# First batch's scores from K and Q as they arrive, splits by halves ahead of the masks, scores of every second slot copied in two

## The chip, the cores and the metric

The kernel runs on one core of a Trainium2 chip, in one launch. The metric is the device time of that core in microseconds (us). Beside the timed runs there is one execution recorded by the hardware profiler; all rows below are from that one. Its engines are TensorE (PE, with PEld for weight loads), VectorE (DVE), ScalarE (ACT), GpSimd (POOL) and SyncE (SP), which issues the transfers.

## The reference

Attention over 8 batches and 8 heads, 576 tokens, 64 dimensions, in which each query keeps only its 32 highest scores, and then a gated chain of matrix products over all 4608 tokens. All inputs are fp32.

```python
scores = (q @ k.transpose(0, 1, 3, 2)) / sqrt(64)        # B=8, H=8, S=576
kth    = np.partition(scores, -32, axis=-1)[..., -32:-31]
scores = np.where(scores >= kth, scores, -1e9)
attn   = np.exp(scores - scores.max(-1, keepdims=True))
attn   = attn / (attn.sum(-1, keepdims=True) + 1e-9)
x      = (attn @ v).transpose(0, 2, 1, 3).reshape(4608, 512)
a, b   = x @ w1, x @ w2                                   # 512 x 1024 each
out    = ((a * b) @ w3) @ w_out                           # 1024 x 1024, 1024 x 512
```

## The kernel before

The work is cut into 144 slots, 18 per batch. A slot is 128 queries of a pair of heads (a few are 64 queries of two pairs), so its scores are a tile `s` of 128 x 2 x 576. Twelve slots give a block of 384 tokens, on which the chain of products runs (tiles `ab` for x@w1 and x@w2, `g` for their product, `eo` for the output; w3 @ w_out is folded into `wf` once, in the first slots).

fp32 accuracy on TensorE is kept by splitting: an operand is written as a high part in fp32r and a low part, the rest, and three products (high-high, low-high, high-low: `PARTS`) stand for one. Q and K come from memory as fp32 into a buffer `raw`, of which there are two, and GpSimd splits them with two instructions into `qt` or `kt`: a CAST for the high part and a TENSOR_TENSOR for the low one (`split_next`, line 218). `load_q` and `load_k` only note what is wanted, `load_next` (line 211) issues the transfer, `load_ahead` (line 223) keeps two under way. A `qt` holds 256 columns and serves two slots, a `kt` 576. Slot 0 alone is scored from the bare fp32 Q and K (`first`, line 613), in one product.

All engines run in the order in which the program is written: a helper class pins every instruction, which is why every row of the profile has its one line, L64, and rows are told apart by the tiles' names. The main loop (line 644) runs over steps p. In a step stand:

- VectorE: the fold of slot p, two tensor_tensor w<-s and two w<-w,s, then top-32 by rounds of MAX8 and MATCH_REPLACE8; the low parts of `x`; the products a * b.
- GpSimd: `edge` and `sums`, then for slot p-1 two masks `pab<-s,pab`, the first of which waits for the last instruction of VectorE's fold; behind the masks the low parts of `g` that are due and one or two splits of a raw Q or K (line 673); in the first slots parts of the weights' decoding.
- ScalarE: the step functions `pab<-s,edge` in front of the masks, the exponentials `pab,sums<-pab,edge`, the normalising `pab<-pab,sums`, and copies out of PSUM (`banks`), the scores' own among them (`take_scores`, line 273).
- TensorE: transposes (`banks<-ident,pab`) and values (`banks<-pab,vt`) of slot p-3, the scores of slot p+2, and in between the chain's products, 12 at a time (`fill`, `SHARES`).

Once the first block has started, the scores of two slots are made in one even step, in two regions of one PSUM tile (`BASES`). The second slot's scores lie in a region that the transposes use too, and are copied in the odd step already (`ahead`, line 711), between the two exponentials. `s` has three buffers. A batch's K is asked for when the last slot that reads the same pair of heads of the batch before is scored (`renew`, line 576).

Of the kernel before, what the change touches and what calls it, by code (L numbers as in the profile page):

```python
# [46 lines left out]
SHARES = (0, 12, 0), (12, 12, 12)  # L47
BASES = (768, 1728), (2304, 192)
TURNED, HOMES = 1024, (0, 2880)
PARTS = (0, 0), (1, 0), (0, 1)  # L50
Q = 256

# [22 lines left out]
def attn_moe(ctx: ExitStack, tc: tile.TileContext, q, k, v, w1, w2, w3, w_out, out, flag, any_missed, general):  # L75
# [120 lines left out]
    def at(x, b, *i):  # L196
        return x[(b, *i)] if isinstance(b, int) else x[(ds(b, 1), *i)].rearrange("o p n -> (o p) n")
# [1 line left out]
    wanted, raws, now = [], [], [0]  # L199

    def load_q(b, t, half):
        qt = att_p.tile([128, 2, Q], F32R, tag="q", name="qt")
        wanted.append((qt, at(q, b, t)[:, half * Q : (half + 1) * Q]))
        return qt

    def load_k(b, hp):
        kt = kv_p.tile([128, 2, S], F32R, tag="k", name="kt")
        wanted.append((kt, at(k, b, hp)))
        return kt

    def load_next():
        to, src = wanted.pop(0)
        raw = raw_p.tile([128, S], F32, tag="raw", name="raw")
        raw = raw[:, : to.shape[-1]]
        sp.dma_start(raw, src)
        raws.append((now[0], raw, to))

    def split_next(engine):
        _, raw, to = raws.pop(0)
        engine.tensor_copy(to[:, 0, :], raw)  # L220
        engine.tensor_tensor(to[:, 1, :], raw, to[:, 0, :].bitcast(F32), op=ALU.subtract)

    def load_ahead():
        while wanted and len(raws) < 2:
            load_next()

    def ready(*tiles):
# [10 lines left out]
    def products_of(cuts, qt, kts, hps):  # L238
        parts = PARTS if qt.dtype == F32R else PARTS[:1]
        for n, (i, j) in enumerate(parts):  # L240
            for a, (dst, lo, hi) in enumerate(cuts):
                rows = HEADS[hps[0] % 2 ^ a] if len(hps) == 1 else slice(0, 128)
                c = (hps[0] + (a if len(hps) == 2 else 0)) * 128 % Q
                pe.matmul(
                    dst, qt[rows, i, c : c + 128], kts[hps[0] // 2 * 2 + a][rows, j, lo:hi],
                    start=n == 0, stop=n == len(parts) - 1,
                )
# [10 lines left out]
    def scores_whole(qt, kts, hps, i):  # L258
        ready(qt, *(kts[hps[0] // 2 * 2 + a] for a in range(2)))
        banks, cuts = late["banks"][:, :], [[], []]  # L260
        for base in BASES[i]:
            n = 512 - base % 512
            for lo, hi in ((0, n), (n, S)):
                cuts[hi - lo < HS].append((banks[:, base + lo : base + hi], lo, hi))
        for cut in cuts:
            products_of(cut, qt, kts, hps)
        apart = BASES[i][1] - BASES[i][0]
        return bass.AP(banks.tensor, banks.offset + BASES[i][0], [banks.ap[0], [apart, 2], [1, S]])

    def new_s():  # L270
        return att_p.tile([128, 2, S], F32, tag="s", name="s", bufs=S_BUFS)

    def take_scores(s, st):
        if not isinstance(st, list):
            act.copy(s, st)
            return
        for src, (lo, hi) in list(zip(st, HALVES))[::-1]:
            act.copy(s[:, :, lo:hi], src[:, :, :HS])

    def top32_steps(s, slot):  # L280
        w = att_p.tile([128, 2, S], F32, tag="w", name="w", bufs=1)
# [291 lines left out]
    def of(table, b):  # L573
        return {hp: table[b, hp] for hp in range(NHP) if (b, hp) in table}

    def renew(table, load, i, last):
        b, hps, _ = slots[i]
        for hp in range(NHP):
            if last[b, hp] == i and b + 1 < B:
                table[b + 1, hp] = load(b + 1, hp)  # L580

    halves, half_at = [], []
    for b, hps, t in slots:
# [4 lines left out]
    def renew_q(g):  # L588
        if g < len(halves):
            qts[g] = load_q(*halves[g])  # L590
# [19 lines left out]
        prefetch(WAITING)  # L610

    now[0] = -4
    first = z_p.tile([128, 3 * CHUNK], F32, tag="z", name="z")
    bare = [first[:, o : o + n].rearrange("p (i c) -> p i c", i=1) for o, n in ((0, S), (S, S), (2 * S, Q))]
    sp.dma_start(bare[2][:, 0], at(q, 0, 0)[:, :Q])
    sp.dma_start(bare[0][:, 0], at(k, 0, 0))
    stir(6)
    prefetch(1)
    sp.dma_start(bare[1][:, 0], at(k, 0, 1))
    for hp in (2, 3):  # L620
        kts[0, hp] = load_k(0, hp)
    prefetch(2)
    load_next()
    prefetch(4)
    load_next()
    renew_q(1)
    for hp in (0, 1):
        kts[0, hp] = kv_p.tile([128, 2, S], F32R, tag="k", name="kt")
    turned, ovs = {}, {}

    def put_back(m):
# [1 line left out]

    def score(h, st):
        b, hps, t = slots[h]
        sts[h] = st(qts[half_at[h]], of(kts, b), hps) if half_at[h] else st(bare[2], bare, hps)

    def scored(h):
        renew(kts, load_k, h, last_pair)
# [4 lines left out]
    for p in range(-2, n_slots + 4):  # L644
        h, i, j, l, m = p + 2, p + 1, p - 1, p - 2, p - 3
        now[0] = p
        if p == 1:
            vts[0, 0] = load_v(0, 0)
            vts[0, 1] = load_v(0, 1)
            vts[0, 2] = load_v(0, 2)  # L650
            vts[0, 3] = load_v(0, 3)
        finder = top32_steps(ss[p], p) if 0 <= p < n_slots else iter(())
        if 0 <= i < n_slots and i not in ss:
            ss[i] = new_s()
            take_scores(ss[i], sts[i])
        for part in fresh:
            split_high(*part)
        if 0 <= j < n_slots:
            edges[j] = edges_of(j)
        if 0 <= l < n_slots:  # L660
            add_up(pabs[l][1])
        folded = next(finder, None)
        for part in fresh:
            split_low(*part)
        fresh.clear()
        take_lasts()
        warm()
        if 0 <= j < n_slots:
            pabs[j] = new_weights()
            for a in range(2):  # L670
                mask(ss[j], edges[j], pabs[j][0], a, folded if a == 0 else None)
        take_lows()
        for _ in range(2 if len(raws) + len(wanted) > 3 else 1):
            if raws and raws[0][0] < p:
                split_next(pool)
        if p == 0:
            raws[:0] = [(-4, bare[hp][:, 0], kts[0, hp]) for hp in range(2)]
        load_ahead()
        warm()
        begin()  # L680
        if p % 2:
            fill(SHARES[1][0])
            evict()
        next(finder, None)
        if 0 <= m < n_slots:
            turned[m] = take_turned(pabs[m][0], *turn(pabs[m][0], None if late else sts[i][1]))
        take_held()
        take_lows()
        if 0 <= l < n_slots:
            invert(pabs[l][1])  # L690
            normalise(*pabs[l])
        if 0 <= j < n_slots:
            exps(edges[j], *pabs[j], 0)
        warm()
        if p == 3:
            stir(6)
        fill(SHARES[p % 2][1])
        next(finder, None)
        warm()
        if h not in sts and (not late or h % 2) and h < n_slots:  # L700
            score(h, (lambda *a: scores_whole(*a, 1)) if late else scores)
            scored(h)
        elif h % 2 == 0:
            for n in (h + 1, h):
                if n < n_slots:
                    score(n, lambda *a, n=n: scores_whole(*a, n % 2))
            for n in (h, h + 1):
                if n < n_slots:
                    scored(n)
        load_ahead()  # L710
        ahead = late and p % 2 == 1 and h < n_slots and h in sts
        if ahead:
            ss[h] = new_s()
            take_scores(ss[h], sts[h])
        if 0 <= j < n_slots:
            exps(edges[j], *pabs[j], 1)
        if 0 <= m < n_slots:
            if not put_back(m):
                for n in [m - 1, m] if put_back(m - 1) else [m]:
                    b, hps, t = slots[n]  # L720
                    ovs[n] = values(of(vts, b), hps, turned.pop(n), n < m)
                    renew(vts, load_v, n, last_use)
        if p == 14:
            stir(9)
        next(finder, None)
        warm()
        for _ in finder:
            pass
        if p % 2:
            hold.append(True)  # L730
        fill(SHARES[p % 2][2])
        hold.clear()
        for d in sorted(ovs):
            b, hps, t = slots[d]
            n = d // BLOCK
            for hp in hps:
                if (n, hp) not in xs:
                    xs[n, hp] = new_x(n)
            fresh += parts_of([xs[n, hp] for hp in hps], column[group_of[d]], t, ovs.pop(d))
            del ss[d], pabs[d], edges[d], sts[d]  # L740
            if (d + 1) % BLOCK == 0:
                starting.append(n)
        if p == 2:
            stir(8)
        warm()
# [73 lines left out]
```

## Time and profile before

| | before |
|---|---|
| time, median of 3 runs (lowest to highest) | 1291.63 us (1289.79 to 1291.91) |
| profiled execution, time | 1289.22 us |
| profiled execution, span | 1287.4 us |
| mean granted TensorE clock | 0.971 of full speed |
| TensorE busy | 1196.6 us (93%), 9867 matmuls |
| VectorE busy | 1159.7 us (90%) |
| ScalarE busy | 1096.2 us (85%) |
| GpSimd busy | 904.9 us (70%) |
| transfers | 62.67 MB, 49 GB/s on average |

Four engines are busy for 70% to 93% of the span, so a share alone doesn't say which of them sets the time of a stretch. Rows are read by stretch and by tile: a row of a timeline gives a start, a duration, the engine, the output tile and the inputs, and in brackets how long that engine was idle just before and on what it waited. The chain that ended last is spread thinly over all of them, its largest entry being 3% for the products into `ab`.

### The profile page before, as it was taken

The page shows a single profiled execution, that of the slowest core. Times are in us where ns is not written, and L with a number is a line of the kernel's source. Part 1 is how long each engine was busy: PE and PEld are TensorE (multiplying, and loading weights), DVE is VectorE, ACT ScalarE, POOL GpSimd, SP SyncE. Part 2 cuts the span into 40 slices and gives each one's busy share as a digit, 9 for nine tenths or more (in the row PEclk, how much of TensorE's full clock was granted, in tenths as well). Part 3 has the DMA queues.
Part 4 walks back from the last instruction along what each step waited for, and adds up shares of the span by engine and source line. Part 5 has one row for each costly group of instructions (what it writes and reads, how often), then busy time and mean ns, then how long its engine had stood idle before and what let it go on. Part 6 is the DMA issues. An engine that isn't in the chain of part 4 may idle for free. (4 is left out here: it accounts for less than half of the span.)

```text
span 1287.4 us, 28209 instructions
## 1 busy us (share of the span) xinstructions
PE 1196.6 (93%) x9867; PEld 1072.3 (83%) x9867; DVE 1159.7 (90%) x3964; ACT 1096.2 (85%) x1974; POOL 904.9 (70%) x1087
## 2 busy tenths in 40 slices
PE   3699789999899999999899999999899999999998
PEld 2445468889889999989889999989889999989898
DVE  7999998898999999999999999999999999999710
ACT  4899987789889999989889999989899999889821
POOL 5887877666867778767867778757867787757410
PEclk6799899999999999999999999999999999999999
DMA  6444401110120011110120021010020021100000
GB/s 221 129 146 155 142 14 47 31 38 20 32 74 15 9 58 48 30 47 11 32 79 9 10 71 39 26 47 15 28 83 10 13 63 38 37 28 2 13 13 26
DMA packets 35878, 62.67 MB, mean 49 GB/s; under 512 B 6036, under 2 KB 22420, under 8 KB 35732
## 3 DMA queue, kind: packets, MB, share of 16 engines
q1 hardware_dynamic: 35732, 60.83, 15.7%
q8 instruction: 78, 1.28, 0.4%
q14 instruction: 68, 0.56, 0.2%
HBM read 51.38 MB, written 9.44 MB: 47 GB/s over the span
## 5 line engine op out<-in xcount | busy, mean ns | idle before, releaser
L64 POOL TENSOR_TENSOR pab<-s,pab 128x576 f32<-128x576 f32 x288 | 407.2, 1436 | 172.4 <-ACT pab L64 74.6
L64 DVE MAX8 top<-w 128x8 f32<-128x192 f32 (+1 forms) x1152 | 466.0, 446 | 0.0
L64 PE MATMUL ab<-x,wh 128*128 128x384 f32 x1536 | 411.7, 348 | 8.3 <-ACT x L64 6.7
L64 DVE MATCH_REPLACE8 w<-top,w 128x192 f32<-128x192 f32 x864 | 289.6, 343 | 0.0
L64 PEld LDWEIGHTS ab<-x,wh 128*128 128x128 f32 x1536 | 272.0, 188 | 20.4 <-ACT x L64 9.2
L64 PE MATMUL ab<-x,wl 128*128 128x384 f32 x768 | 260.2, 339 | 0.0
L64 ACT ACTIVATE pab<-pab,edge 128x576 f32<-128x576 f32 x288 | 222.2, 773 | 1.3 <-POOL pab L64 1.3
L64 ACT ACTIVATE pab<-s,edge 128x576 f32<-128x576 f32 x288 | 209.0, 781 | 14.1 <-POOL edge L64 13.9
L64 PE MATMUL eo<-g,wf 128*128 128x384 f32 x1152 | 220.1, 344 | 0.3 <-ACT asb L64 0.3
L64 ACT ACTIVATE pab<-pab,sums 128x576 f32<-128x576 f32 x288 | 208.3, 775 | 5.5 <-DVE sums L64 5.5
L64 PEld LDWEIGHTS eo<-g,wf 128*128 128x128 f32 x1152 | 199.8, 188 | 4.2 <-issue 3.4
L64 ACT COPY s<-banks 128x1152 f32<-128x1152 f32 x127 | 141.5, 1114 | 46.8 <-PE banks L64 46.6
L64 ACT COPY pab<-banks 128x1152 f32<-128x1152 f32 x132 | 147.2, 1115 | 35.5 <-PE banks L64 20.8
L64 DVE TENSOR_TENSOR w<-s 128x384 f32<-128x384 f32 x288 | 164.3, 611 | 10.8 <-ACT s L64 9.3
L64 PE MATMUL banks<-ident,pab 128*128 128x128 f32 x1188 | 157.0, 278 | 14.7 <-DVE x L64 6.1
L64 PEld LDWEIGHTS banks<-ident,pab 128*128 128x128 f32 x1188 | 129.3, 141 | 47.8 <-ACT s L64 28.1
L64 DVE TENSOR_TENSOR w<-w,s 128x384 f32<-128x384 f32 x288 | 162.8, 565 | 4.9
L64 PE MATMUL banks<-pab,vt 128*64 128x128 f32 (+1 forms) x2960 | 161.7, 266 | 0.8 <-ACT pab L64 0.8
L64 PEld LDWEIGHTS banks<-pab,vt 128*64 128x64 f32 x2960 | 146.6, 138 | 10.4 <-ACT pab L64 1.4
L64 PE MATMUL banks<-kt,qt 64*128 64x320 f32 (+1 forms) x1524 | 134.0, 307 | 12.8 <-ACT pab L64 7.2
L64 PEld LDWEIGHTS banks<-kt,qt 64*128 64x128 f32 (+1 forms) x1524 | 120.2, 191 | 29.6 <-issue 11.5
L64 PEld LDWEIGHTS ab<-x,wl 128*128 128x128 f32 x768 | 144.5, 188 | 0.0
(67 smaller groups left out, 1295.3 us busy)
## 6 DMA issues: line engine op xcount, KB each, us to landing
z<-in_w SPq DMA_DIRECT2D x32, 512.0 KB, 3.9
vt<-in_v SPq DMA_DIRECT2D x32, 320.0 KB, 3.4
raw<-in_q SPq DMA_DIRECT2D x79, 128.0 KB, 2.2
raw<-in_k SPq DMA_DIRECT2D x30, 288.0 KB, 2.9
out_t<-osb SPq DMA_DIRECT2D x32, 192.0 KB, 1.9
z<-in_wo SPq DMA_DIRECT2D x8, 512.0 KB, 5.4
out_t<-osb SPq DMA_DIRECT2D x16, 160.0 KB, 1.8
z<-in_k SPq DMA_DIRECT2D x2, 288.0 KB, 3.7
```

Source lines behind the costliest of these rows:

```text
L64: ins = fn(*args, **kw)
```

## The change

The change has three parts.

1. Batch 0 is scored throughout from fp32 Q and K, in one product instead of three. Both are loaded straight into `qt` and `kt` tiles, so GpSimd splits nothing of batch 0. The first two K come as transfers of 64 partitions each, the two halves that slot 0 reads first, the others behind the first weights. Four K of batch 0 share two buffers of the pool, which leaves two free: two K of batch 1 are asked for at step 6 (`EARLY_K`), the others when batch 0's are used up.
2. A raw K is entered as two pieces of 288 columns (`cuts_of`), and one due piece, or one Q, is split in every step ahead of the masks (`split_due`); a second follows behind the masks where more than four units are pending, a wanted tile counted twice.
3. The scores of a slot that is made in the second place of its pair are copied by two instructions of 128 x 576, one ahead of the second exponential and one behind it, instead of one of 128 x 1152 ahead of it.

```diff
--- before.py
+++ after.py
@@ -47,6 +47,7 @@
 SHARES = (0, 12, 0), (12, 12, 12)
 BASES = (768, 1728), (2304, 192)
 TURNED, HOMES = 1024, (0, 2880)
+EARLY_K = 6
 PARTS = (0, 0), (1, 0), (0, 1)
 Q = 256
 
@@ -199,8 +200,13 @@
     wanted, raws, now = [], [], [0]
 
     def load_q(b, t, half):
-        qt = att_p.tile([128, 2, Q], F32R, tag="q", name="qt")
-        wanted.append((qt, at(q, b, t)[:, half * Q : (half + 1) * Q]))
+        src = at(q, b, t)[:, half * Q : (half + 1) * Q]
+        if isinstance(b, int) and b == 0:
+            qt = att_p.tile([128, 2, Q], F32, tag="q", name="qt")
+            sp.dma_start(qt[:, 0, :], src)
+        else:
+            qt = att_p.tile([128, 2, Q], F32R, tag="q", name="qt")
+            wanted.append((qt, src))
         return qt
 
     def load_k(b, hp):
@@ -213,15 +219,24 @@
         raw = raw_p.tile([128, S], F32, tag="raw", name="raw")
         raw = raw[:, : to.shape[-1]]
         sp.dma_start(raw, src)
-        raws.append((now[0], raw, to))
+        raws.extend(cuts_of(raw, to, now[0]))
+
+    def cuts_of(raw, to, since):
+        n = to.shape[-1]
+        return [(since, raw, to, lo, lo + HS if n == S else n) for lo in range(0, n, HS)]
 
     def split_next(engine):
-        _, raw, to = raws.pop(0)
-        engine.tensor_copy(to[:, 0, :], raw)
-        engine.tensor_tensor(to[:, 1, :], raw, to[:, 0, :].bitcast(F32), op=ALU.subtract)
+        _, raw, to, lo, hi = raws.pop(0)
+        engine.tensor_copy(to[:, 0, lo:hi], raw[:, lo:hi])
+        engine.tensor_tensor(to[:, 1, lo:hi], raw[:, lo:hi], to[:, 0, lo:hi].bitcast(F32), op=ALU.subtract)
+
+    def split_due(most):
+        while raws and raws[0][0] < now[0] and most:
+            split_next(pool)
+            most -= 1
 
     def load_ahead():
-        while wanted and len(raws) < 2:
+        while wanted and len({id(r[2]) for r in raws}) < 2:
             load_next()
 
     def ready(*tiles):
@@ -264,18 +279,23 @@
                 cuts[hi - lo < HS].append((banks[:, base + lo : base + hi], lo, hi))
         for cut in cuts:
             products_of(cut, qt, kts, hps)
+        if i:
+            return tuple(banks[:, base : base + S] for base in BASES[i])
         apart = BASES[i][1] - BASES[i][0]
         return bass.AP(banks.tensor, banks.offset + BASES[i][0], [banks.ap[0], [apart, 2], [1, S]])
 
     def new_s():
         return att_p.tile([128, 2, S], F32, tag="s", name="s", bufs=S_BUFS)
 
-    def take_scores(s, st):
-        if not isinstance(st, list):
+    def take_scores(s, st, heads=(0, 1)):
+        if isinstance(st, list):
+            for src, (lo, hi) in list(zip(st, HALVES))[::-1]:
+                act.copy(s[:, :, lo:hi], src[:, :, :HS])
+        elif isinstance(st, tuple):
+            for a in heads:
+                act.copy(s[:, a, :], st[a])
+        else:
             act.copy(s, st)
-            return
-        for src, (lo, hi) in list(zip(st, HALVES))[::-1]:
-            act.copy(s[:, :, lo:hi], src[:, :, :HS])
 
     def top32_steps(s, slot):
         w = att_p.tile([128, 2, S], F32, tag="w", name="w", bufs=1)
@@ -577,7 +597,10 @@
         b, hps, _ = slots[i]
         for hp in range(NHP):
             if last[b, hp] == i and b + 1 < B:
-                table[b + 1, hp] = load(b + 1, hp)
+                if table is not kts or b:
+                    table[b + 1, hp] = load(b + 1, hp)
+                elif hp % 2:
+                    kts[1, 2 + hp // 2] = load_k(1, 2 + hp // 2)
 
     halves, half_at = [], []
     for b, hps, t in slots:
@@ -610,22 +633,26 @@
         prefetch(WAITING)
 
     now[0] = -4
-    first = z_p.tile([128, 3 * CHUNK], F32, tag="z", name="z")
-    bare = [first[:, o : o + n].rearrange("p (i c) -> p i c", i=1) for o, n in ((0, S), (S, S), (2 * S, Q))]
-    sp.dma_start(bare[2][:, 0], at(q, 0, 0)[:, :Q])
-    sp.dma_start(bare[0][:, 0], at(k, 0, 0))
+    for pair in range(2):
+        whole = kv_p.tile([128, 2, S], F32, tag="k", name="kt")
+        for n in range(2):
+            kts[0, 2 * pair + n] = whole[:, n : n + 1, :]
+
+    def fill_k(hp, rows):
+        sp.dma_start(kts[0, hp][rows, 0, :], at(k, 0, hp)[rows, :])
+
+    renew_q(0)
+    fill_k(0, HEADS[0])
+    fill_k(1, HEADS[1])
     stir(6)
     prefetch(1)
-    sp.dma_start(bare[1][:, 0], at(k, 0, 1))
-    for hp in (2, 3):
-        kts[0, hp] = load_k(0, hp)
+    fill_k(0, HEADS[1])
+    fill_k(1, HEADS[0])
     prefetch(2)
-    load_next()
+    fill_k(2, slice(0, 128))
+    fill_k(3, slice(0, 128))
     prefetch(4)
-    load_next()
     renew_q(1)
-    for hp in (0, 1):
-        kts[0, hp] = kv_p.tile([128, 2, S], F32R, tag="k", name="kt")
     turned, ovs = {}, {}
 
     def put_back(m):
@@ -633,7 +660,7 @@
 
     def score(h, st):
         b, hps, t = slots[h]
-        sts[h] = st(qts[half_at[h]], of(kts, b), hps) if half_at[h] else st(bare[2], bare, hps)
+        sts[h] = st(qts[half_at[h]], of(kts, b), hps)
 
     def scored(h):
         renew(kts, load_k, h, last_pair)
@@ -665,16 +692,18 @@
         fresh.clear()
         take_lasts()
         warm()
+        behind = len(raws) + 2 * len(wanted) > 4
+        split_due(1)
         if 0 <= j < n_slots:
             pabs[j] = new_weights()
             for a in range(2):
                 mask(ss[j], edges[j], pabs[j][0], a, folded if a == 0 else None)
         take_lows()
-        for _ in range(2 if len(raws) + len(wanted) > 3 else 1):
-            if raws and raws[0][0] < p:
-                split_next(pool)
-        if p == 0:
-            raws[:0] = [(-4, bare[hp][:, 0], kts[0, hp]) for hp in range(2)]
+        if behind:
+            split_due(1)
+        if p == EARLY_K:
+            for hp in range(2):
+                kts[1, hp] = load_k(1, hp)
         load_ahead()
         warm()
         begin()
@@ -711,9 +740,11 @@
         ahead = late and p % 2 == 1 and h < n_slots and h in sts
         if ahead:
             ss[h] = new_s()
-            take_scores(ss[h], sts[h])
+            take_scores(ss[h], sts[h], (0,))
         if 0 <= j < n_slots:
             exps(edges[j], *pabs[j], 1)
+        if ahead:
+            take_scores(ss[h], sts[h], (1,))
         if 0 <= m < n_slots:
             if not put_back(m):
                 for n in [m - 1, m] if put_back(m - 1) else [m]:
```

The first place is GpSimd at the start, ahead of slot 0's masks; `wo` is a decoded weight, `edge` and `over` belong to slot 0. Before:

```order
13 L64 CAST kt<-raw 128x576
14 L64 TENSOR_TENSOR kt<-raw,kt 128x576
15 L64 CAST kt<-raw 128x576
16 L64 TENSOR_TENSOR kt<-raw,kt 128x576
17 L64 CAST qt<-raw 128x256
18 L64 TENSOR_TENSOR qt<-raw,qt 128x256
19 L64 TENSOR_TENSOR wo<-z 128x512 x2
20 L64 TENSOR_TENSOR edge<-top_102,coef 128x4
21 L64 TENSOR_TENSOR over<-top_102 128x2
22 L64 TENSOR_TENSOR pab<-s,pab 128x576 x2
```

The same place after:

```order
13 L65 TENSOR_TENSOR wo<-z 128x512 x2
14 L65 TENSOR_TENSOR edge<-top_102,coef 128x4
15 L65 TENSOR_TENSOR over<-top_102 128x2
16 L65 TENSOR_TENSOR pab<-s,pab 128x576 x2
17 L65 TENSOR_TENSOR wo<-z 128x512 x3
```

The six instructions that split two K and a Q are gone; what follows them keeps its order.

The second place is GpSimd in the steps about the change from batch 0 to batch 1 (slots 18 and 19), with the split of a Q; `sums` and `pab` belong to the attention slots, `g` to the chain of products. Before:

```order
147 L64 TENSOR_TENSOR edge<-top_104,coef 128x4
148 L64 TENSOR_TENSOR over<-top_104 128x2
149 L64 TENSOR_SCALAR sums<-sums 128x2
150 L64 TENSOR_TENSOR pab<-s,pab 128x576 x2
151 L64 CAST qt<-raw 128x256
152 L64 TENSOR_TENSOR qt<-raw,qt 128x256
153 L64 TENSOR_TENSOR g<-asb,g 128x384
```

After:

```order
128 L65 TENSOR_TENSOR edge<-top_104,coef 128x4
129 L65 TENSOR_TENSOR over<-top_104 128x2
130 L65 TENSOR_SCALAR sums<-sums 128x2
131 L65 CAST qt<-raw 128x256
132 L65 TENSOR_TENSOR qt<-raw,qt 128x256
133 L65 TENSOR_TENSOR pab<-s,pab 128x576 x2
134 L65 TENSOR_TENSOR g<-asb,g 128x384
```

The Q's two instructions stand ahead of the two masks instead of behind them. In the whole program 64 Q and 37 halves of K stand so, and 6 Q and 19 halves behind the masks; before, 79 Q and 32 whole K stood behind them. TensorE's queue differs in batch 0's scores alone, 12 matmuls of a slot becoming 4; VectorE's is the same.

The third place is ScalarE in an odd step; `pab,sums<-pab,edge` are the two exponentials, `s<-banks` is the copy of the scores. Before:

```order
432 L64 COPY pab<-banks 128x1152
433 L64 ACTIVATE pab<-pab,sums 128x576 x2
434 L64 ACTIVATE pab,sums<-pab,edge 128x576
435 L64 COPY s<-banks 128x1152
436 L64 ACTIVATE pab,sums<-pab,edge 128x576
437 L64 ACTIVATE pab<-s,edge 128x576 x2
```

After:

```order
448 L65 COPY pab<-banks 128x1152
449 L65 ACTIVATE pab<-pab,sums 128x576 x2
450 L65 ACTIVATE pab,sums<-pab,edge 128x576
451 L65 COPY s<-banks 128x576
452 L65 ACTIVATE pab,sums<-pab,edge 128x576
453 L65 COPY s<-banks 128x576
454 L65 ACTIVATE pab<-s,edge 128x576 x2
```

The second exponential, whose mask it waits for, stands between the two pieces instead of behind the whole copy. The next transposes write to the region that the first piece frees.

## Rows read from the trace of the kernel before

**Rows 1.** Stretches: from:to, length, busy (count) PE PEld DVE ACT POOL, clock, DMA, GB/s.
```profile
146.52:203.99 57.47, 45.02 (x374) 37.59 (x374) 54.60 (x176) 49.65 (x94) 46.57 (x53) 0.88 0.17 50
203.99:259.55 55.56, 50.49 (x392) 46.30 (x390) 46.12 (x163) 43.78 (x78) 37.81 (x48) 0.94 0.13 37
308.54:359.66 51.12, 47.23 (x392) 43.48 (x390) 48.84 (x164) 43.75 (x78) 42.08 (x47) 0.97 0.10 26
405.81:453.08 47.27, 46.89 (x392) 43.56 (x390) 45.53 (x163) 43.63 (x78) 36.87 (x41) 1.00 0.04 10
872.88:922.10 49.22, 45.55 (x396) 42.12 (x392) 47.97 (x164) 43.93 (x79) 41.06 (x46) 1.00 0.09 25
```
**Rows 2.** Timeline of the start: start, duration, engine, operation, count, [idle before <- releaser].
```profile
2.23 0.43 SPq L64 DMA_DIRECT2D z<-in_k  x1
...
4.60 1.27 PE L64 MATMUL st<-z 64*128 64x288 f32 x2
...
6.84 1.23 PE L64 MATMUL st<-z 64*128 64x288 f32 x6 [0.98 <-DMA z<-in_k]
...
9.33 2.66 DVE L64 TENSOR_TENSOR w<-s 128x384 f32<-128x384 f32 x2 [9.33 <-ACT s L64]
...
9.99 1.58 POOL L64 TENSOR_TENSOR kt<-raw,kt 128x576 fp32r<-128x576 f32 x1
```
**Rows 3.** Timeline of VectorE in slot 3.
```profile
42.10 2.15 DVE L64 TENSOR_TENSOR w<-s 128x384 f32<-128x384 f32 x2
...
52.13 0.69 DVE L64 SCALAR_TENSOR_TENSOR z<-z,t 128x512 int32<-128x512 int32 x1 [0.73 <-ACT z L64]
```
**Rows 4.** Timeline from slot 17 to slot 21, batch 0 to batch 1.
```profile
193.27 2.67 DVE L64 TENSOR_TENSOR w<-s 128x384 f32<-128x384 f32 x2
...
210.02 0.41 PE L64 MATMUL banks<-kt,qt 64*128 64x320 f32 x2 [2.31 <-POOL qt L64]
...
229.01 0.56 PE L64 MATMUL banks<-kt,qt 128*128 128x320 f32 x2 [1.73 <-POOL qt L64]
...
229.83 4.68 PE L64 MATMUL banks<-kt,qt 128*128 128x320 f32 x22 [0.26 <-POOL qt L64]
...
238.44 0.49 DVE L64 TENSOR_TENSOR x<-banks,x 128x128 fp32r<-128x128 f32 x2 [5.43 <-ACT x L64]
```
**Rows 5.** Timeline of a usual slot, and of one with early sums (507).
```profile
413.31 1.43 POOL L64 TENSOR_SCALAR sums<-sums 128x2 f32<-128x2 f32 x1
...
414.11 1.15 DVE L64 TENSOR_TENSOR w<-w,s 128x384 f32<-128x384 f32 x2
...
415.97 2.81 POOL L64 TENSOR_TENSOR pab<-s,pab 128x576 f32<-128x576 f32 x2 [1.23 <-PE ab L64]
...
419.50 0.76 ACT L64 ACTIVATE pab<-pab,edge 128x576 f32<-128x576 f32 x1
...
419.71 0.39 POOL L64 CAST qt<-raw 128x256 fp32r<-128x256 f32 x1
...
420.19 0.74 POOL L64 TENSOR_TENSOR qt<-raw,qt 128x256 fp32r<-128x256 f32 x1
...
420.26 1.11 ACT L64 COPY s<-banks 128x1152 f32<-128x1152 f32 x1
...
507.57 1.01 DVE L64 TENSOR_TENSOR w<-s 128x384 f32<-128x384 f32 x2
...
507.79 0.40 POOL L64 TENSOR_SCALAR sums<-sums 128x2 f32<-128x2 f32 x1
```
**Rows 6.** Timeline of a slot in which a K is split.
```profile
340.57 1.01 DVE L64 TENSOR_TENSOR w<-s 128x384 f32<-128x384 f32 x2
...
340.71 2.63 POOL L64 TENSOR_TENSOR kt<-raw,kt 128x576 fp32r<-128x576 f32 x1
...
341.51 2.25 DVE L64 TENSOR_TENSOR w<-w,s 128x384 f32<-128x384 f32 x2
```
**Rows 7.** Waits: engine, tile, releaser, us in total, times, longest.
```profile
PEld banks L64 <- ACT s L64: 28.1, 63, 0.5
```

## The prediction

> **What bounds the kernel.** I read the stretches first. A slot is one step of the main loop; VectorE opens it with its fold, four tensor_tensor instructions over the scores. In the steady part (slots 42 to 47, the row from 405.81 in [rows 1]) six slots last 47.27 us, TensorE is busy for 46.89 of them and VectorE for 45.53: TensorE is the bound, and VectorE has 1.74 to spare. Other stretches are longer with no more TensorE work: slots 18 to 23 (from 203.99) take 55.56 us with VectorE idle for 9.44 and the clock at 0.94, so partly at 1.2 instead of 2.4 GHz; slots 30 to 35 (from 308.54) take 51.12 with TensorE idle for 3.89; the stretch from 872.88 takes 49.22 with 3.67 idle. So time can be had in three places: the start, the change from batch 0 to batch 1, and the slots in which K is split. In the start VectorE is the bound, with one wait in slots 0 to 6. The timelines of those places came next, engine beside engine: one looks for a wait, then for what its releaser waited for.
>
> **The start.** Slot 0 needs Q and two heads of K. Before, the second head waits for a whole K whose issue comes at 2.23, behind 512 KB of weights, and TensorE goes on at 6.84 [rows 2]. Now the two half transfers that slot 0 needs go first, one issue (0.43) more than the first K, so both heads are there at about 4.60 + 0.45 = 5.05. Four score products follow, the first at the lower clock: 1.27 + 0.9 gives 7.2, where before 6.84 + 1.23 = 8.07 ended them. I take 1.0 off, between 0 and 1.8 (the whole 6.84 − 5.05).
> By the Trainium skill, SBUF — State Buffer, "Can I just issue two DMAs to hit both halves?", two transfers on the two halves of the partitions share the same engines and go one behind the other, and each alone reaches half the ports. By that rule the second half would land no earlier than the second K does now, and the sum would lose this 1.0. No row here shows a transfer of 64 partitions.
>
> **Splits of batch 0.** They go altogether. VectorE's first fold pair took 2.66 us with the tensor_tensor of kt beside it [rows 2]; an undisturbed pair takes 1.01 [rows 5]: 1.6 off. In slot 3 GpSimd was late by its splits: the pair took 2.15, and a wait of 0.73 for ScalarE's z followed at 52.13 [rows 3]: 1.8 off. Batch 0's scores become one fp32 product instead of three; in these slots TensorE waits for others, so I count nothing for it, and a loss of as much as 0.5 per slot would still be hidden there.
> Instead four half splits of the next K stand in steps 7 to 10 ahead of the masks. A Q of 256 columns costs 0.39 + 0.74 = 1.13 [rows 5], a half of 288 at most 1.13 × 288 / 256 = 1.27; I use 1.25. In these steps VectorE has no slack and GpSimd is early, so they can stand beside the fold: 0 to 4 × 1.25 = 5.0; I take 3 on. Their two loads, issued in step 6 between weight loads, cost SP 2 × 0.43; weights are fetched three units ahead, which hides it (0.9 without).
>
> **Batch 0 to batch 1.** Twice TensorE waits for a Q split that GpSimd does behind its two masks: 2.31 us until 210.02, and 1.73 until 229.01; the second time the scores ran to 229.83 + 4.68 = 234.5, and VectorE stood 5.43 us waiting for x, which needs the products behind them [rows 4]. The usual order of a slot is sums, masks 2.81, qt [rows 5]: ahead of the masks the Q is ready some 3 us earlier, and both waits go. Its CAST then waits for the load and for TensorE's last read of the buffer with the masks queued behind it; both come a slot earlier unless TensorE is late. What is left is TensorE's own row, as in the usual six slots: 55.56 − 47.27 = 8.3; I take 7.5 off (3 to 8.3). In slots 12 to 17 VectorE idles 57.47 − 54.60 = 2.87 [rows 1], and its fold pair at 193.27 took 2.67 instead of 1.01 [rows 4, 5], 4.5 together; GpSimd is relieved there too (halves, two K earlier): 2.7 off, 0 to 4.
>
> **The K slots of batches 2, 4 and 6.** A K split behind the masks runs into the next fold: the tensor_tensor of kt took 2.63, where one of the masks, as long, takes 1.4 [rows 5, 6], and the second fold pair 2.25 instead of 1.15. So it is in several slots of each such stretch. With 45.55 us of TensorE's work per six slots from 872.88 [rows 1] 51.12 − 45.55 = 5.6 can be had in the first (part of TensorE's busy time there is at the lower clock) and 3.7 in each of the others: 13.0. It doesn't all go: in one step of each stretch two halves and a g still follow each other, 1.25 + 2.8 + 1.25 + 1.0 = 6.3 on GpSimd behind sums that end 2.1 into a slot of 7.4 to 7.9, so it is about 1.2 late again. Three times 1.2 stays: 9 off (2 to 13).
>
> **The copy in two pieces.** 63 copies of 1.11 [rows 5] become pairs. The trace of before has no such pair; by the two masks in a row (2.81 for two) pieces add little: between 0 and, if each cost a 256-column CAST's 0.39 more, 25 us on ScalarE, near the lower end since ScalarE's instructions overlap. It hides in ScalarE's idle time (47.27 − 43.63 = 3.6 in six slots with three copies, so 1.2 for each). The first piece needs mask 0 alone, and the transposes, which waited 63 times for the whole copy [rows 7], now wait for the first piece. TensorE's whole idle time in the steady stretch, 0.38 for three such waits, can be this: 0.127 × 63 = 8.0 at most. VectorE is near, so I take 3 off (0 to 8).
>
> **What the splits ahead cost.** 64 Q and 37 halves of K now stand between sums and the masks, while VectorE folds. Usually sums are held until 414.74, and the fold's last instruction begins about then (its second pair runs from 414.11 to 415.26) [rows 5]. A split behind them comes after it and delays no fold; the masks then start up to 0.6 later, and exp has that: mask 0 is done by 415.97 + 1.4 = 417.4, exp 0 begins at 419.50. But where sums come early (done at 508.19 in a fold that began at 507.57 [rows 5]; 14 such slots in the trace), the split meets the running fold and holds up one or two instructions, 0.4 to 1.25. GpSimd is earlier now, so I count some 20 of the 101: 8 to 25 us, of which VectorE's 1.74 per six slots takes up a part. I take 5 on (0 to 118: 64 × 1.13 + 37 × 1.25).
>
> **Sum.** −1.0 − 1.6 − 1.8 + 3 − 7.5 − 2.7 − 9 − 3 + 5 = −18.6 on the profiled execution's 1289.22: 1270.6. The median of the three runs, 1291.63, stands 2.4 above that execution; I forecast 1271.
>
> **Rivals.**
> Full gain: sums stay late, no split meets a fold, TensorE's idle time goes: without the +3 and +5, and with 11 and 5 for K slots and copy, −30.6: 1258.6. For it: the fold of 413 held GpSimd off until its third instruction was done. Against: the 14 early slots.
> Seam only: in the K slots the lateness moves from behind the masks to before them, and TensorE's short waits stay. Left are 1.0 + 1.6 + 1.8 + 7.5 + 2.7 − 3 = 11.6: 1277.6. For it: two halves of K are no less work than a whole. Against: they are spread over more slots.
> Slower: the splits ahead meet the folds as a rule. Place: the fold of every slot with a split; price 1.13 or 1.25. Without such meetings in the steady part the sum is −23.6, and VectorE's slack over 120 steady slots is 20 × 1.74 = 35, so this decides from about (23.6 + 35) / 1.17 = 50 of the 101 on; with three quarters (76) it is 89 − 58.6 = +30: 1320. For it: at 340.71 a kt that came 0.14 us into a fold took the last instruction's turn, and the pair lost 1.1. Against: sums usually end behind the third.
> The Trainium skill, SBUF — State Buffer, "Who interferes with whom", says of these two kinds of instruction that VectorE with two inputs in SBUF and GpSimd reading SBUF exclude each other for a whole instruction, whichever starts first. By that rule, which the kt of 340.71 bears out, it comes to this rival wherever sums are done before the fold's third instruction.
>
> **Chances.** Forecast 0.50, full gain 0.22, seam only 0.14, slower 0.14. A change under 0.2% can't be told from none here; of the slower case a part lies within it, of seam only and forecast a little. Faster 0.82, same 0.07, slower 0.11. The range 1255 to 1288 takes in the first three and leaves most of the last out.
>
> **What would show it.** Start: VectorE's first fold at 8.0 to 8.6, its pair at 1.0. Seam: no wait of TensorE for qt, slots 18 to 23 in 47 to 49 us at clock 1.0. K slots: six-slot stretches of 47 to 48. Copy: the transposes' waits for s gone. Splits ahead: long fold pairs in slots with early sums alone; more than 50 of them, or usual six slots above 47.3, or a first fold later than 9.3 would make the forecast wrong.

## The result: 18.5 us slower

| | before | after |
|---|---|---|
| median, same chip (lowest to highest, 4 runs each) | 1290.71 us (1287.84 to 1291.91) | 1309.22 us (1308.45 to 1310.37) |
| profiled execution: span | 1287.4 us | 1308.6 us |
| mean granted TensorE clock | 0.971 | 0.989 |
| TensorE busy | 1196.6 us | 1192.4 us |
| VectorE busy | 1159.7 us | 1157.2 us |
| ScalarE busy | 1096.2 us | 1107.3 us |
| GpSimd busy | 904.9 us | 910.4 us |

The ratio is 1.0147, interval 1.0128 to 1.0167. The forecast was 1271, with a range to 1288: wrong in its sign. TensorE and VectorE have no more to do, ScalarE, which is idle for 15% of the span, has 11 us more, and the clock is higher; so the time went into waiting. Measured from the starts of VectorE's folds, the two spans differ as follows.

| slots | after minus before, us |
|---|---|
| up to the first fold | −0.9 |
| 0 to 6 | −3.2 |
| 7 to 11 | +1.9 |
| 12 to 17 | −1.2 |
| 18 to 23 (batch 0 to 1) | −6.0 |
| 30 to 35, 66 to 71, 102 to 107 (K slots) | −6.7 |
| all other slots from 24 to 142, and the tail | +37.2 |

Where a gain was forecast there is one. What was not forecast is the last row: in the usual slots, most groups of six lose 1.9 to 2.4 us. The stretches of the changed kernel that answer to the first four rows of [rows 1], slots 12, 18, 30 and 42 on, columns as there:

```profile
144.32:200.62 56.30, 45.36 (x358) 36.70 (x358) 52.42 (x175) 49.66 (x96) 42.33 (x50) 0.88 0.12 38
200.62:250.20 49.58, 46.79 (x392) 43.63 (x390) 45.55 (x163) 44.22 (x81) 39.08 (x46) 1.00 0.13 38
300.04:348.31 48.27, 45.48 (x392) 41.97 (x390) 47.24 (x164) 44.20 (x81) 42.64 (x52) 1.00 0.07 19
396.77:446.35 49.58, 46.78 (x392) 43.62 (x390) 45.56 (x164) 44.23 (x81) 34.85 (x40) 1.00 0.02 7
```

Read the last: TensorE has the same work in six usual slots (46.78 against 46.89) but 2.80 us of idle time where it had 0.38. Something makes TensorE, which bounds these slots, wait. The waits of the whole execution name it (engine, tile, releaser, us in total, times, longest); the first of these rows answers to [rows 7]:

```profile
PEld banks L65 <- ACT s L65: 79.0, 63, 1.3
ACT s L65 <- PE banks L65: 76.2, 63, 2.2
PE banks L65 <- ACT s L65: 58.7, 63, 0.9
```

The prediction wanted these 63 waits to go. They have nearly trebled, and the row of TensorE's matmuls, absent before, is now 0.9 each. The timeline of one odd step, the columns as in [rows 2], answers to the copy in [rows 5]; `ident` marks the transposes:

```profile
411.27 0.77 ACT L65 ACTIVATE pab<-pab,edge 128x576 f32<-128x576 f32 x1
411.93 0.19 ACT L65 ACTIVATION_READ_ACCUMULATOR pab<-pab,edge 128x1 f32 x1
412.03 0.62 ACT L65 COPY s<-banks 128x576 f32<-128x576 f32 x1
...
412.55 0.78 ACT L65 ACTIVATE pab<-pab,edge 128x576 f32<-128x576 f32 x1
...
413.22 0.20 ACT L65 ACTIVATION_READ_ACCUMULATOR pab<-pab,edge 128x1 f32 x1
413.31 0.63 ACT L65 COPY s<-banks 128x576 f32<-128x576 f32 x1
...
414.00 1.20 PE L65 MATMUL banks<-ident,pab 128*128 128x128 f32 x9 [0.93 <-ACT s L65]
```

The transposes do not begin when the first piece is done, at 412.65, but 0.06 us after the second, at 413.94. Between the pieces stands the second exponential. From the start of the first read of the scores to the end of the last it now takes 1.91 us, before 1.11: 0.80 more, and the engine that waits for it, TensorE, has no slack.

### The profile page after: what moved, and what is told of

The parts are those of the page before. It is cut to its first block, busy times and chain, and to the rows that moved or that the text cites. A ratio compares the mean times of both kernels' runs of the same rounds, so it can differ in the third digit from the quotient of the medians.

```text
span 1308.6 us, 28237 instructions
## 1 busy us (share of the span) xinstructions
PE 1192.4 (91%) x9803; PEld 1066.0 (81%) x9803; DVE 1157.2 (88%) x3964; ACT 1107.3 (85%) x2038; POOL 910.4 (70%) x1117
## 5 line engine op out<-in xcount | busy, mean ns | idle before, releaser
L65 ACT COPY s<-banks 128x576 f32<-128x576 f32 x191 | 150.6, 789 | 76.3 <-PE banks L65 76.2
L65 DVE TENSOR_TENSOR w<-w,s 128x384 f32<-128x384 f32 x288 | 169.5, 589 | 4.9
L65 DVE TENSOR_TENSOR w<-s 128x384 f32<-128x384 f32 x288 | 154.2, 576 | 11.2 <-ACT s L65 8.4
L65 POOL TENSOR_TENSOR edge<-top,coef 128x4 f32<-128x4 f32 x144 | 42.9, 298 | 128.9 <-DVE top L65 127.8
L65 PE MATMUL banks<-kt,qt 64*128 64x320 f32 (+1 forms) x1520 | 128.7, 301 | 0.0
```

Of the source, the lines that this page charges most:

```text
L65: ins = fn(*args, **kw)
```

## Experiments

Each was timed in rounds with the kernel before, and its ratio is to that kernel. The theory after the result, called late release: the transposes wait for the last read of the PSUM tile `banks`, and the change moved that read behind an exponential. Its rivals: the splits ahead of the masks do the harm; or two instructions on ScalarE cost more than one.

**One copy again.**

```diff
-        if i:
-            return tuple(banks[:, base : base + S] for base in BASES[i])
...
-            take_scores(ss[h], sts[h], (0,))
+            take_scores(ss[h], sts[h])
         if 0 <= j < n_slots:
             exps(edges[j], *pabs[j], 1)
-        if ahead:
-            take_scores(ss[h], sts[h], (1,))
```

> The changed kernel with the scores of every second slot copied by one instruction again, ahead of the second exponential, as before; the rest of the change stands. Late release (the transposes of the next slot wait for the last piece of the copy, which now stands behind an exponential): the 63 waits of about 0.8 us go, 63 x 0.77 = 48 us at most, so 1260 to 1272, and six usual slots go back from 49.6 to about 47.3. Splits ahead (the splits ahead of the masks hold up folds and masks): the copy is not the cause, 1303 to 1310, and six usual slots stay at 49 to 50.

1270.42 us (1264.56 to 1271.18), ratio to before 0.9832 [0.9799, 0.9864]; a second time, beside the last experiments, 1268.12, 0.9841 [0.9824, 0.9859]. The rest of the change is worth 19 to 21 us; the copy alone takes that away and as much again. Six usual slots (42 to 47, second run):

```profile
387.81:435.07 47.26, 46.91 (x392) 43.60 (x390) 45.52 (x164) 43.61 (x78) 33.39 (x40) 1.00 0.02 7
```

Back to the length of before, with the splits still ahead of the masks: they cost these slots nothing. They are not free everywhere: slots 54 to 59, 90 to 95 and 126 to 131, each behind a change of batch, take 48.2 where they took 47.3, and the six ahead of each of them 46.5 instead of 47.1. The expectation for the second run, which came 0.9 under it:

> The kernel with one copy ahead once more, beside the one above on the same chip: 1269 to 1271.

**The copy in pieces alone**, put into the kernel before, by the same lines.

> The kernel before with the copy in two pieces alone, the second behind the second exponential. Late release: 0.77 us per odd slot, a little less where the K slots already wait: 1290.7 + 40 = 1331 (1320 to 1339). Splits ahead: within 5 us of before, 1286 to 1296.

1325.16 us (1324.18 to 1327.03), 1.0269 [1.0245, 1.0292]: 36 us slower than before, without any other part of the change.

**The second piece from another source.**

```diff
-            take_scores(ss[h], sts[h], (1,))
+            act.copy(ss[h][:, 1, :], ss[i][:, 1, :])
```

The second head's scores of these slots are then left out; those of the slot before stand in their place.

> The changed kernel, with the second piece reading head 1 of the slot before from its tile of scores instead of the PSUM tile; so these slots work on another head's scores. Instruction count, order and piece sizes stay. As built, the transposes then wait for the first piece. Late release: 1258 to 1270, as with one copy or a little better. Piece cost (two instructions take ScalarE more time than one, 2 x 0.6 to 0.8 against 1.1): 1300 to 1310, as the changed kernel. Splits ahead: 1305 to 1310.

1268.60 us (1268.04 to 1269.76), 0.9836 [0.9813, 0.9858]. The pieces, their order and their place behind the exponential are those of the changed kernel; only the second no longer reads `banks`. An odd step of it:

```profile
402.67 0.62 ACT L65 COPY s<-banks 128x576 f32<-128x576 f32 x1
403.19 0.78 ACT L65 ACTIVATE pab<-pab,edge 128x576 f32<-128x576 f32 x1
...
403.54 1.15 PE L65 MATMUL banks<-ident,pab 128*128 128x128 f32 x9
...
403.96 0.66 ACT L65 COPY s<-s 128x576 f32<-128x576 f32 x1
```

Now the transposes start 0.25 us after the first piece and before the second, without a wait. So it is the tile's last read that they wait for in the changed kernel, and the 40 us are that wait. It also answers a question the prediction left in its sum: with the release even earlier than before, so that the 63 waits are gone altogether, six usual slots last 47.43 us, not less than 47.27. Nothing was to be had there.

**Both pieces ahead of the exponential.**

```diff
-            take_scores(ss[h], sts[h], (0,))
+            take_scores(ss[h], sts[h])
         if 0 <= j < n_slots:
             exps(edges[j], *pabs[j], 1)
-        if ahead:
-            take_scores(ss[h], sts[h], (1,))
```

> The changed kernel with both pieces ahead of the second exponential. Late release: the last piece ends about 0.1 to 0.2 us later than one whole copy did, so 63 x 0.15 = 9 us over the kernel with one copy: 1265 to 1280. Piece cost: 1300 to 1310. Splits ahead: 1303 to 1310.

1269.08 us (1266.82 to 1272.08), 0.9840 [0.9811, 0.9868]: as with one copy. Usual slots are 0.17 us longer per six than with one; two pieces as such cost next to nothing, less than was expected.

**One copy, behind the exponential.**

```diff
-        if i:
-            return tuple(banks[:, base : base + S] for base in BASES[i])
...
-            take_scores(ss[h], sts[h], (0,))
         if 0 <= j < n_slots:
             exps(edges[j], *pabs[j], 1)
         if ahead:
-            take_scores(ss[h], sts[h], (1,))
+            take_scores(ss[h], sts[h])
```

> The changed kernel with one whole copy of the scores, placed behind the second exponential. Late release (it matters where the last read of the PSUM tile stands): the copy ends about where the second of two pieces ended, so the transposes wait some 0.8 to 0.9 us 63 times: 1270 + 0.8 x 63 = 1320 (1305 to 1328), six usual slots at 49 to 50. Piece count (two instructions are the matter): 1267 to 1274, as with one copy ahead.

1305.34 us (1304.66 to 1307.41), 1.0125 [1.0108, 1.0142]. One instruction in the late place does what two did: 35 to 37 us over the same copy in the early place. The mechanism is shown from both sides. The size is at the lower edge of what was expected, for the wait is not paid in full where something else is late as well: in slots 30 to 35 the changed kernel is only 1.3 us longer than with one copy, not 2.3.

The rest of the change was then taken apart, always with one copy, made as above; the code that follows shows the rest alone. Splits can be whole or by halves, behind or ahead of the masks.

**Whole and behind** (what is left is the start and the early K).

```diff
-        return [(since, raw, to, lo, lo + HS if n == S else n) for lo in range(0, n, HS)]
+        return [(since, raw, to, 0, n)]
...
-        behind = len(raws) + 2 * len(wanted) > 4
-        split_due(1)
...
-        if behind:
-            split_due(1)
+        split_due(2 if len(raws) + len(wanted) > 3 else 1)
```

The first `split_due` stands ahead of the masks, the second behind them.

> One copy ahead; batch 0 unsplit, the half loads and the early K as in the change; but a K is split whole and all splits stand behind the masks, by the rule of before. Position (what GpSimd does ahead of the masks gives the gain at the change of batch and in the K slots): only the start's 4.4 us and a part of slots 12 to 17 are left, 1282 to 1287. Early loads (the gain comes from batch 0 having no splits and K coming early): 1268 to 1275.

1277.14 us (1276.27 to 1280.63), 0.9917 [0.9899, 0.9936]: neither theory's, but between them. Slots 18 to 23 and 30 to 35:

```profile
199.00:246.26 47.26, 46.90 (x392) 43.58 (x390) 45.51 (x163) 43.59 (x78) 35.28 (x44) 1.00 0.14 40
293.67:344.39 50.72, 47.04 (x392) 43.38 (x390) 48.80 (x163) 43.69 (x78) 42.04 (x47) 0.97 0.09 27
```

The change of batch is already a usual stretch, with every Q behind its masks; the K slots are as before. So the two gains have two causes.

**Halves and behind.**

```diff
-        split_due(1)
...
-        if behind:
-            split_due(1)
+        split_due(2 if behind else 1)
```

> One copy ahead; K split by halves, but all splits behind the masks, two in a step where the change's rule says so. Position: TensorE waits for qt at the change of batch as before, and halves of K behind the masks run into the next fold: 1279 to 1286. Halves (smaller pieces spread over more slots are what helps, wherever they stand): 1268 to 1274.

1324.91 us (1322.75 to 1325.17), 1.0274 [1.0257, 1.0291]: both theories missed. Cut in halves, a K takes two steps unless the rule grants a second unit, and the Q behind it in the queue comes late; TensorE's matmuls into `banks` wait for it 24 times, in the kernel before 6 times for 5.7 us in all, with whole K behind the masks never:

```profile
PEld banks L65 <- POOL qt L65: 36.2, 24, 3.3
PE banks L65 <- POOL qt L65: 29.0, 24, 3.0
```

**Whole and ahead.**

```diff
-        return [(since, raw, to, lo, lo + HS if n == S else n) for lo in range(0, n, HS)]
+        return [(since, raw, to, 0, n)]
```

> One copy ahead; splits ahead of the masks as in the change, but a K whole, 2.4 us of GpSimd in one step. Position: 1267 to 1273, as with halves, since a split behind sums meets no fold. Halves: a whole K holds up the masks by 1.25 more and meets the fold's end, in some 20 to 30 steps: 1276 to 1290.

1269.00 us (1267.60 to 1271.07), 0.9851 [0.9834, 0.9867]. With a whole K in one step it is as fast as with halves (1268 to 1270): ahead of the masks, the halves bring nothing that these times show, and for whole K the place is worth 8 us (1277.14 behind them). Slots 30 to 35 take 47.69, with halves 46.93; slots 54 to 59 and their like give about half of that back (47.8 for 48.2).

**K ahead, Q behind.**

```diff
-        split_due(1)
+        k_next = bool(raws) and raws[0][2].shape[-1] == S
+        split_due(1 if k_next else 0)
...
-        if behind:
+        if behind or not k_next:
```

> One copy ahead, as in x1_one_copy; a half of a K is split ahead of the masks, a Q behind them as before the change. Position by need (the K slots gain from splits ahead, the slots with a Q alone do not, and lose where sums come early): the stretches from slots 54, 90 and 126 go back from 48.2 to 47.3, the K slots stay at 46.9, so some 2 us under one copy: 1266 to 1269. Position throughout (the Q ahead is what took TensorE's waits for qt away at the change of batch): slots 18 to 23 rise to 50 or more, 1272 to 1278.

1306.80 us (1306.01 to 1308.22), 1.0136 [1.0115, 1.0156]. Both totals missed, though slots 18 to 23 rise to 53.71, as the second theory said; it is the backlog of halves again, 24 waits of TensorE for qt, 25.6 us. With halves, a Q is just in time only because it stands ahead of the masks.

**The first K loaded whole.**

```diff
-    fill_k(0, HEADS[0])
-    fill_k(1, HEADS[1])
+    fill_k(0, slice(0, 128))
+    fill_k(1, slice(0, 128))
...
-    fill_k(0, HEADS[1])
-    fill_k(1, HEADS[0])
```

> One copy ahead; the first two K loaded whole, 128 partitions each, instead of by halves. Ports (a transfer of 64 partitions gains nothing over one of 128): the first fold begins within 0.3 us of that with halves, total 1268 to 1272. Bytes (the halves bring what slot 0 needs with half the traffic): TensorE waits for the second K up to 1 us, the first fold later by 0.5 to 1.0, total 1270 to 1273.

1265.38 us (1263.88 to 1267.22), 0.9821 [0.9801, 0.9841]. Both too high, and the interval meets that of the same kernel with halves. Its first fold begins at 7.51, and in the next kernel, also loaded whole, at 9.20; with halves it came between 7.50 and 8.41 in the executions profiled here. In all of them slot 0's score products start at 4.59 or 4.60; they take 1.66 and 3.35 with whole loads, 1.65 to 2.56 with halves, and the fold follows some 1.3 later. A microsecond at the start thus can't be laid to either way of loading. The first two K transfers, up to 2.6 us, of the changed kernel and then of this one (count, KB each, us from issue to landing):

```profile
kt<-in_k SPq DMA_DIRECT2D x2, 144.0 KB, 2.9
```

```profile
kt<-in_k SPq DMA_DIRECT2D x2, 288.0 KB, 3.1
```

Twice the bytes on twice the partitions land 0.2 us later, in the next kernel, by the same two transfers, 0.5 (3.4). The halves bring nothing that these runs can show; that both K go ahead of the weights does not depend on them.

**Early splits behind the masks**, in steps up to 11, added to the last.

```diff
-        split_due(1)
+        split_due(1 if p > 11 else 0)
...
-        if behind:
+        if behind or p <= 11:
```

> One copy ahead and the first K loaded whole, as in y7_whole_loads; and in the steps up to 11 the four halves of K are split behind the masks. Meeting the fold (in these steps sums are early and the half meets the running fold, 0.6 us in each of slots 7 to 10): slots 7 to 11 go from 59.6 back to 57.7 us, the total to 1262 to 1265. Later backlog (a half that waits behind the masks holds up what follows on GpSimd): slots 7 to 11 stay at 59 or more, 1265 to 1268.

1265.29 us (1264.35 to 1266.84), 0.9797 [0.9780, 0.9814]. Slots 7 to 11 take 57.73 as the first theory said, the total is that of the second: slots 12 to 17 (57.49 against 56.03) give most of it back. What is left is under what these runs can tell. This and the one above are the fastest, 2% under before.

## Why the prediction was wrong

**The step that failed: the copy in two pieces.** It said that "the transposes, which waited 63 times for the whole copy, now wait for the first piece", and took 3 us off, "0 to 8". Measured: 39 to 41 us on (1309.2 against 1270.4 and 1268.1), 36 when done alone. The order of ScalarE's queue was in view, with an exponential between the pieces. Had the last read been taken as the one that counts, the exponential's 0.76 [rows 5] times 63 would have given 48 us on; the changed kernel's rows give 1.91 − 1.11 = 0.80, times 63 is 50, and both are upper bounds. The range left that end out without a reason, for it allowed no loss. The section on the change says that the transposes write to the region that the first piece frees, and the one on the kernel before that they use the region of these scores; both are wrong. They write columns 1024 to 2176 of the tile (`TURNED`), the pieces lie in 2304 to 2880 and 192 to 768 (`BASES`): they meet neither, and wait all the same, for the tile's last read. By which rule the program comes to hold that wait is not shown.

**The other steps**, read from the kernel with one copy, come to −18.6 and −20.9 us; the forecast without the copy was −15.6.

- Start: right in size as far as it can be told. The first fold came at 8.41 (8.0 to 8.6 was said), in the other executions with this start between 7.50 and 8.37, with the start of before at 9.33 and, with the copy in pieces alone, 10.32. The loss that the prediction worked out for the two half transfers did not come: slot 0's products run on from 4.60, where they had stood 0.98 for the second K [rows 2]. The pair took 1.03; slots 0 to 2 became 1.3 shorter (1.6 said), but with one copy 0.0 and 1.5, so that much is no more than the spread. Slots 3 to 6 gained 1.96 (1.8 said). The row that answers to VectorE's in [rows 2]:

```profile
8.41 1.03 DVE L65 TENSOR_TENSOR w<-s 128x384 f32<-128x384 f32 x2 [8.41 <-ACT s L65]
```

- Halves in steps 7 to 10: +1.9, +3 said. Each pair of the fold took 1.68 instead of 1.0 beside a half of K, as here in slot 7 (GpSimd, then VectorE):

```profile
84.47 0.42 POOL L65 CAST kt<-raw 128x288 fp32r<-128x288 f32 x1
84.98 0.98 POOL L65 TENSOR_TENSOR kt<-raw,kt 128x288 fp32r<-128x288 f32 x1
```

```profile
84.70 1.68 DVE L65 TENSOR_TENSOR w<-s 128x384 f32<-128x384 f32 x2
```

- Batch 0 to batch 1: −7.75 with one copy, −7.5 said. The reason given is half of it. With halves the place ahead of the masks is needed: with the Q alone behind them (K ahead, Q behind) TensorE waits for qt there again, 1.74 us twice where it had been 2.31 and 1.73, and slots 18 to 23 are nearly as long as before:

```profile
202.30:256.01 53.71, 49.22 (x392) 45.10 (x390) 45.53 (x163) 43.65 (x78) 36.84 (x47) 0.97 0.13 38
```

But with whole splits behind the masks the stretch is 47.26 as well, so against the kernel before it is not the place that frees TensorE. What does is among the parts kept there: batch 0 without splits and the early K. Which of the two it is was not tried. That the size came out so closely is in part luck.
- Slots 12 to 17: −0.7 and −1.3 in the two executions with one copy, −2.7 said: over-sized, within its range.
- K slots: −4.2, −4.0 and −2.6, 10.7 in all, 9 said. Here the place ahead of the masks is the cause, as said: with whole splits behind them slots 30 to 35 stay at 50.7. The sum has two slips. It took the second stretch to be as long as the third; it lasted 50.86, so 5.3 could be had there instead of 3.7. And 2.1 + 6.3 in a slot of 7.4 to 7.9 is 0.5 to 1.0 late, not 1.2. Put right, both would have raised the 9; what stayed was 1.4 in each stretch (46.93 against 45.55).
- Splits ahead of the masks: some 20 meetings with a fold were counted on. In the kernel with one copy an instruction of VectorE ran 0.4 us or more over its usual time in 25 slots (counted in its trace, the last slot left out), four of them slots 7 to 10. In the kernel before there are 23 such slots, most of them those in which a K is split: the splits ahead moved the meetings more than they added any. The slots from 24 on outside the K stretches lost 2.9 us together, 1.3 in the second execution (+5 said).

**The rivals.** The slower one named 1320 and its place was the fold. The sign came true, the mechanism did not: with one copy as many splits stand ahead of the masks, and the kernel is faster than before. Its chance, 0.14, was for something else. The rival that was missing is a slower one by the change's third part.

## What to carry to other kernels

When a read is cut in two, ask which piece the next writer waits for and what stands between the two on their engine. Here the release moved to the last one, and that the columns do not overlap was no proof that there is no wait. Give every edit's range an end on the losing side, above all where the waiting engine is the bound: here a delay of 0.8 us, 63 times, cost 39 to 41 of 50. Smaller units of work are only as good as the rule that grants them turns: halves doubled the queue's length in steps, and where they stood behind the masks they cost 48 us against whole ones.

## What was not expected of the chip

Cutting a copy cost far less than feared: two of 128x576 took 0.62 and 0.63 us where one of 128x1152 took 1.11. They overlap: with both ahead of the exponential the two last 1.16 us together, 0.05 more than the one. A transfer of 144 KB to 64 partitions landed in 2.9 us, one of 288 KB to 128 partitions, in the same place, in 3.1 and 3.4; the Trainium skill, SBUF — State Buffer, "Can I just issue two DMAs to hit both halves?", says that only one transfer over all partitions uses all ports. These rows agree, but they do not show it: a time that hardly depends on the bytes would look alike.
